# Down projection of the last 1024 tokens: 12 of 28 K tiles by Strassen's scheme for three of four token pairs

## The chip, the cores and the metric

The kernel runs on one core of one Trainium2 chip. The metric is the device time of one execution in microseconds. A core has TensorE (PE in the profile; matmuls, and PEld for the loads of their stationary operand), VectorE (DVE), ScalarE (ACT), GpSimd (POOL) and SyncE (SP, which here issues nearly all DMA transfers). Each engine works off its own queue in order. SBUF is the working memory, PSUM the memory that matmuls write, eight banks of 512 float32 columns.

## The reference

One transformer block on 2048 tokens of width 1024: a conditioned layer norm, linear attention, and a gated FFN of width 3584, both with residuals. What the change touches is the last product.

```python
def _B_ref(x, w_gate, w_up, w_down):
    return _gelu(x @ w_gate) * (x @ w_up) @ w_down

x = x + ga * _A_ref(h, A_wqkv, A_wo)
h = _layernorm(x, axis=-1) * (1 + cb) + sb
x = x + gb * _B_ref(h, B_w_gate, B_w_up, B_w_down)      # w_down: 3584 x 1024, bfloat16
```

## The kernel before

**Tiling.** The 2048 tokens are 16 chunks of 128 (`c_`). The FFN works in two passes `p` of eight chunks each (1024 tokens). A pass has 14 units `u`; a unit makes two of the 28 tiles `fc` (128 wide) of the hidden width, for 1024 tokens, and leaves them in `YT` (bf16). A unit already uses Strassen's scheme in Winograd's form: seven products `P1` to `P7`, each in two halves `t` (gate, up) of four matmuls. P1 and P2 are bf16; P5, P6, P7, P3 and P4 work on sums of operands in float32 that TensorE reads as `f32r`. VectorE makes the sums of the tokens (`s_sum`, line 1371, once a pass) and of the weights (`t_sum`, line 1391, for the next unit); ScalarE converts one more (`A22R`, line 1357, and line 1380). In PSUM, P1 opens a bank, ScalarE copies it to a second bank (`pcp`, line 1421), P6 and P7 add to the copy, and VectorE adds the copy and P5 (`padd`, line 1427, with P5 in `ES`). Then Gelu (line 1432, ScalarE, into `GE`) and the product with the other half (line 1436, VectorE, into `YT`).

**Down projection.** After the units of a pass, `down` (line 1501) multiplies `YT` with `w_down`, which comes in seven groups `WDT[q]` of four K tiles (1 MB each; `wd_dma`, line 1325). Group 2 is loaded in unit 12, groups 5, 3, 6, 4 at the end of a pass, each as soon as the tile it overwrites has been read; groups 0 and 1 stay from the first pass. A chunk takes two banks (`2 * (c_ % 4)`, 512 columns each) and 28 matmuls for each. `evac` (lines 1493, 1494, 1496) multiplies by `GBB`, adds the residual in `XALL` and writes the result to memory.

In the second pass the first four chunks go together, group by group; the next three go one after the other, all 28 K tiles each; the last chunk goes in column pieces of 512, 320, 128 and 64:

```python
                for c_ in gb_[:-1]:
                    down_q(c_, range(7), first=True, last=True)
                c_ = NCH - 1
                for k, (b, k0, k1) in enumerate(((6, 0, 512), (7, 512, 832), (0, 832, 960), (1, 960, 1024))):
                    down(c_, k, b, k0, k1, list(range(NFC)), True, True)
                    evac(c_, k, b, k0, k1)
```

**What sets the order.** Every instruction is recorded by `sch.op` with the bytes that it reads and writes; from these the waits between engines are made. The order on each engine's queue is the order in which the program records, except in one early segment that a planner (`reorder`) sorts, and which ends in the second unit of the first pass. SBUF is one arena with offsets by hand, and tiles overlay each other: `SS` (sums of tokens), `TP` (sums of weights), `WT`, `H2`, `GE`, `ES` belong to the FFN, `XALL` holds the tokens' residuals and results.

Of the kernel before, what the change touches and what calls it, by code (L numbers as in the profile page):

```python
# [6 lines left out]
dt = mybir.dt  # L7
# [3 lines left out]
P = 128  # L11
# [50 lines left out]
OFF_XL = [OFF_GUH + i * 2048 for i in range(4)]  # L62
NXR = 7
OFF_KVT = OFF_GUH + 2048


class Op:
# [246 lines left out]
def bass_adaLN_cond__linear_attn_block__geglu_ffn__prompt_kernel(  # L314
# [16 lines left out]
    with ExitStack() as es:  # L331
# [6 lines left out]
        def at(name, shape, dty, off):  # L338
            return nc.alloc_sbuf_tensor_at(name, shape, dty, offset=ABASE + off, align_bytes=4)
# [22 lines left out]
        W2 = at("w2", [P, NG, D], bf16, OFF_WK)  # L362
        WDQ = [HBO[1], HBO[2], OFF_WS, OFF_WS + 8192, HBO[0], OFF_TP[0], OFF_TP[2]]
        WDT = [at(f"wd{q}", [P, 4, D], bf16, WDQ[q]) for q in range(7)]
        PK = [at(f"pk{i}", [P, D], bf16, OFF_PK[i]) for i in range(NCH)]
        MB = [at(f"mb{i}", [P, D], bf16, OFF_MB[i]) for i in range(NG)]
        MTB = [at(f"mtb{i}", [P, NDC, P], bf16, OFF_MTB[i]) for i in range(2)]
# [136 lines left out]
        def yrow(fc):  # L504
            return fc + 16 if fc < 12 else fc - 12
# [723 lines left out]
        def pq_scale(sg, h, gs):  # L1229
            i, t0 = sg % 2, h * HW  # L1230
            for g0, g1 in gs:
                ap = PQ[sg][:, g0:g1, t0:t0 + HW]
                rng = r_pq(sg, g0, g1, t0, t0 + HW)
                sch.op(V, lambda e, ap=ap, i=i, h=h, g0=g0, g1=g1: e.tensor_tensor(ap, ap, RB[i][:, h, g0:g1, :], ALU.mult),  # L1234
                       rd=rng + r_rb(i, h, g0, g1), wr=rng, deps=rb_ops[sg, h], note=f"pqs{sg}.{h}.{g0}")
# [100 lines left out]
        def ln2_stats(c_, on_act):  # L1336
            i = c_ % 4
            if on_act:
                ln_stats_act(c_, XL[i], r_2k(OFF_XL[i], f"xl{i}"), 1)
            else:  # L1340
                ln_stats(c_, "B")
                ln_nm(c_)

        def ln2_rows(c_):
            i = c_ % 4
            b_, rng = XL[i], r_2k(OFF_XL[i], f"xl{i}")
            xhat_act(c_, b_, rng)
            h, ci = divmod(c_ % (2 * CPG), CPG)
            tdma(Q, H2[h][:, :, ci * P:(ci + 1) * P], b_[:, :], rng, r_h2(h, 0, NDC, ci * P, (ci + 1) * P), f"T2 {c_}")
# [10 lines left out]
        def s_sum(p, i, j):  # L1360
            a, b = H2
            k0, k1, s0, s1 = (2 * j, 2 * j + 2, 0, SGW) if i == 3 else (0, ND2, j * 2 * P, (j + 1) * 2 * P)
            lo = lambda t_: (t_[:, k0:k1, s0:s1])
            hi = lambda t_: (t_[:, ND2 + k0:ND2 + k1, s0:s1])
            rl = lambda h: r_h2(h, k0, k1, s0, s1)
            rh = lambda h: r_h2(h, ND2 + k0, ND2 + k1, s0, s1)
            in0, in1, op, rd = ((lo(b), hi(b), ALU.add, rl(1) + rh(1)),
                                (lo(S32[0]), lo(a), ALU.subtract, r_ss(0, k0, k1, s0, s1) + rl(0)),
                                (lo(a), lo(b), ALU.subtract, rl(0) + rl(1)),
                                (hi(a), lo(S32[1]), ALU.subtract, rh(0) + r_ss(1, k0, k1, s0, s1)))[i]  # L1370
            sch.op(V, lambda e: e.tensor_tensor(SS[i][:, k0:k1, s0:s1], in0, in1, op), rd=rd, wr=r_ss(i, k0, k1, s0, s1), note=f"ssum{i} {p}.{j}")  # L1371
# [63 lines left out]
        def y_out(i, b, fc, h):  # L1435
            sch.op(V, lambda e: e.tensor_tensor(YT[:, yrow(fc), h * SGW:(h + 1) * SGW], GE[i][:, :], PS(b + 1), ALU.mult),  # L1436
                   rd=r_2k(OFF_GE[i], f"ge{i}"), prd=pr(b + 1), wr=r_yt(fc, h * SGW, (h + 1) * SGW), note="yT")
# [3 lines left out]
        def unit(p, u, order=(1, 5, 6, 2, 7, 3, 4)):  # L1441
            more = u + 1 < NFP
            f1, f2 = 2 * u, 2 * u + 1
            done = set()
            for k in order:
                if isinstance(k, tuple):
                    wo_chunk(*k)
                    continue
                if callable(k):
                    k()  # L1450
                    continue
                late = p == u == 0 and k == 2
                gb_, gk, yf, yh = (None, 1, 0, 0) if late else {2: (BA, 0, f1, 0), 7: (BE, 1, f2, 1), 3: (BC, 0, f2, 0), 4: (BB, 0, f1, 1)}.get(k, (None, 1, 0, 0))
                for t in range(2):
                    prod(u, t, k)
                    if k == 1:
                        if held[0]:
                            held[0]()
                            held[0] = None
                        pcp(t)  # L1460
                    elif k == 5:
                        escp(t)
                    elif k == 6:
                        padd(t, BC)
                    elif k == 7:
                        padd(t, BE)
                    if gb_ is not None and t == gk:
                        gelu(gb_)
                        ig = (gi[0] - 1) % 2
                done.add(k)  # L1470
                if k == 2 and u + 2 < NFP:
                    wt_dma(u + 2)
                if k == 4:
                    held[0] = lambda: y_out(ig, BB, f1, 1)
                elif gb_ is not None:
                    y_out(ig, gb_, yf, yh)
                if k == 1:
                    if p == u == 0:
                        ar_copy(0)
                    elif u > 0:  # L1480
                        t_sum(u, 4)
                if more:
                    if k == (3 if p == u == 0 else 5):
                        t_sum(u + 1, 0)
                    if k == (3 if p == u == 0 else 2):
                        t_sum(u + 1, 1)
                    if k == 3:
                        t_sum(u + 1, 3)
                        t_sum(u + 1, 2)
# [24 lines left out]
                    evac(c_, k, b + k, k * 512, (k + 1) * 512)  # L1514

        pq_scale(2, 0, GH[0] + GH[1])
        mark.append(sch.n)
        def cb1():
            sch.op(V, lambda e: e.tensor_scalar(CB1T[:, :], CBT[:, :], 1.0, None, op0=ALU.add), rd=r_sm("cbT"), wr=r_sm("cb1T"))
# [15 lines left out]
        for c_ in range(2, 14):  # L1535
# [4 lines left out]
            if c_ < 10:  # L1540
                ln2_rows(c_ - 2)
            SLOT[c_]()
        ORD0 = (1, 2, 5, 6, lambda: (s_sum(0, 2, 1), gelu(BA)), (14, BE),
                lambda: (y_out(0, BA, 0, 0), s_sum(0, 3, 0), s_sum(0, 3, 1)), 7, (15, BA), 3, 4)
        for p in range(2):
            c0 = p * 2 * CPG
            for u in range(NFP):
                unit(p, u, *([ORD0] if p == u == 0 else []))
                if p == 0 and u == 1:
                    mark.append(sch.n)  # L1550
                if p == 0 and u in (2, 4):
                    wd_dma(u // 2 - 1)
                if u == NFP - 2:
                    wd_dma(2)
            held[0]()
            held[0] = None
            for q in (5, 3, 6, 4):
                wd_dma(q)
            ga_, gb_ = range(c0, c0 + CPG), range(c0 + CPG, c0 + 2 * CPG)
            for c_ in (c0, c0 + 3, c0 + 1, c0 + 2):  # L1560
                down_q(c_, (0,), first=True)
            for q in (1, 2, 3, 5):
                for c_ in ga_:
                    down_q(c_, (q,))
            if p == 0:
                for c_ in range(2 * CPG, NCH):
                    ln2_stats(c_, False)
                    ln2_rows(c_)
                    if c_ == 3 * CPG - 1:
                        mod2_act(0)  # L1570
                    if c_ == NCH - 3:
                        mod2(1, 0, 2)
            for c_ in ga_:
                down_q(c_, (6, 4), last=True)
            if p == 0:
                mod2(1, 2, 2)
                for i, j in ((0, 0), (0, 1), (1, 0), (1, 1), (2, 0), (2, 1), (3, 0), (3, 1)):
                    s_sum(1, i, j)
                for c_ in gb_:
                    down_q(c_, (2, 3), first=True)  # L1580
                wt_dma(0)
                wt_dma(1)
                for q in (4, 5, 6):
                    for c_ in gb_:
                        down_q(c_, (q,))
                    if q == 4:
                        ar_copy(1)
                for k in range(5):
                    t_sum(0, k)
                for c_ in gb_:  # L1590
                    down_q(c_, (0, 1), last=True)
            else:
                for c_ in gb_[:-1]:
                    down_q(c_, range(7), first=True, last=True)
                c_ = NCH - 1
                for k, (b, k0, k1) in enumerate(((6, 0, 512), (7, 512, 832), (0, 832, 960), (1, 960, 1024))):
                    down(c_, k, b, k0, k1, list(range(NFC)), True, True)
                    evac(c_, k, b, k0, k1)


        sch.reorder(mark[0], mark[1], (DVE_, ACT_, POOL_), {id(x4_op): 8.0})
# [73 lines left out]
```

## Time and profile before

| | us |
|---|---|
| median of 3 runs (lowest, highest) | 801.89 (801.64, 802.12) |
| the profiled execution, its own time | 801.02 |
| its span, first to last instruction | 798.9 |
| granted TensorE clock, mean over the span | 1.00 of full speed |
| VectorE busy from 700 to 799 us, by tens | 0, 0, 0, 3.9, 7.3, 1.8, 2.4, 2.8, 1.6, 3.3 |
| TensorE busy from 700 to 799 us, by tens | 10 in each, 6.0 in the last 9 us |
| ScalarE busy from 700 to 799 us | 0 |

A group's duration is that of one instruction from its start to its end. Matmuls overlap, so their spacing is shorter than their duration; it is read from a stretch of the chain of waits, divided by the count. The chain of waits follows the run back from its last instruction, at each step to what released it.

### The profile page before, as it was taken

Reading aid. Unit: us, or ns where it says so; the run is one execution under the profiler, and the core shown is the slowest. Engines: PE = TensorE matmul, PEld = TensorE weight load, DVE = VectorE, ACT = ScalarE, POOL = GpSimd, SP = SyncE. Lnnn points to the kernel's source line nnn. Section 1 sums busy time; section 2 is a strip of 40 time slices with the busy share of each in tenths; the row PEclk is TensorE's granted clock in tenths of the full one; section 3 lists DMA queues with packets and bytes.
Section 4 is the critical chain, followed back from the end, with each engine's and each line's share of the span. In section 5 each row is a group of like instructions: output and inputs, shape, how many; then the busy total and the mean of one; then the engine's idle time right before and its main releaser. Section 6 shows DMA issues by size and latency. Waiting matters only on the chain.

```text
span 798.9 us, 10878 instructions
## 1 busy us (share of the span) xinstructions
PE 792.2 (99%) x4029; PEld 466.0 (58%) x4029; DVE 568.5 (71%) x1008; ACT 302.9 (38%) x511; POOL 40.3 (5%) x102
## 2 busy tenths in 40 slices
PE   8999999999999999999999999999999999999998
PEld 4444445665445776777765444467677777744445
DVE  6799898884989987878876373578887878601422
ACT  2597743232573444435443401034444435300000
POOL 2131200000410000000001000000000000000000
PEclk9999999999999999999999999999999999999999
DMA  9789849849996153323319234023132332430100
GB/s 285 242 179 231 176 110 237 201 95 200 225 268 166 54 158 105 106 71 89 102 56 250 39 80 106 27 80 105 54 105 58 102 90 68 144 120 7 53 21 27
DMA packets 161340, 97.73 MB, mean 122 GB/s; under 512 B 68476, under 2 KB 148612, under 8 KB 160264
## 3 DMA queue, kind: packets, MB, share of 16 engines
q1 hardware_dynamic: 161272, 97.04, 47.4%
q8 instruction: 32, 0.52, 0.3%
q14 instruction: 20, 0.16, 0.1%
q10 hardware_dynamic: 16, 0.00, 0.0%
HBM read 78.92 MB, written 4.47 MB: 104 GB/s over the span
## 4 chain that ended last, share of the span: by engine, by line
PE 92%; DVE 3%; DMA 2%; SPq 1%; issue 1%; ACT 0%; POOL 0%; POOLq 0%; DVEq 0%
PE ps_all L1416 44%; PE ps_all L1501 24%; PE ps_all L873 7%; PE ps_all L909 7%; PE ps_all L858 7%; PE ps_all L1242 2%; DMA wmq<-in_w_mod_dram 1%; DVE xall L1256 1%; DMA wt<-in_B_w_up_dram 1%; SPq L680 1%; DVE tp L1391 0%; PE ps_all L891 0%; PE ps_all L1174 0%; PE ps_all L744 0%; DVE pq L1234 0%
## 5 line engine op out<-in xcount | busy, mean ns | idle before, releaser
L1416 PE MATMUL ps_all<-ss,tp 128*128 128x512 f32 x896 | 224.3, 402 | 0.2 <-DVE ss L1371 0.2
L1501 PE MATMUL ps_all<-wd,yT 128*128 128x512 bf16 (+3 forms) x952 | 193.9, 366 | 0.0
L1416 PEld LDWEIGHTS ps_all<-ss,tp 128*128 128x128 f32 x896 | 168.3, 188 | 40.8 <-DVE ss L1371 0.9
L1501 PEld LDWEIGHTS ps_all<-wd,yT 128*128 128x128 bf16 x952 | 90.0, 98 | 103.8 <-ACT ge L1432 0.5
L1432 ACT ACTIVATE ge<-ps_all 128x512 f32<-128x512 f32 x112 | 64.2, 598 | 143.7 <-DVE ps_all L1427 80.2
L1416 PE MATMUL ps_all<-h2a,wt 128*128 128x512 bf16 x448 | 106.2, 380 | 0.0
L1391 DVE TENSOR_TENSOR tp<-wt 128x512 fp32r<-128x512 bf16 x112 | 74.5, 689 | 41.9 <-PE ps_all L1416 20.6
L1436 DVE TENSOR_TENSOR yT<-ge,ps_all 128x512 bf16<-128x512 f32 x112 | 74.6, 685 | 34.3 <-PE ps_all L1416 30.9
L1427 DVE TENSOR_TENSOR ps_all<-ps_all,es 128x512 f32<-128x512 f32 x112 | 75.3, 696 | 16.0 <-PE ps_all L1416 16.0
L1493 DVE TENSOR_TENSOR ps_all<-ps_all,gbb 128x512 f32<-128x512 f32 (+3 forms) x34 | 22.7, 668 | 79.0 <-PE ps_all L1501 79.0
L1391 DVE TENSOR_TENSOR tp<-wt,tp 128x512 fp32r<-128x512 bf16 x112 | 72.1, 685 | 0.0
L1416 PEld LDWEIGHTS ps_all<-h2a,wt 128*128 128x128 bf16 x448 | 39.4, 98 | 54.3 <-issue 13.9
L858 PE MATMUL ps_all<-wk,h1T 128*128 128x512 bf16 x248 | 56.7, 379 | 0.4 <-DVE h1T L701 0.4
L909 PE MATMUL ps_all<-h1T,wq 128*128 128x512 bf16 x256 | 56.7, 379 | 0.0
L1242 PE MATMUL ps_all<-w,pq 128*128 128x512 bf16 x256 | 56.3, 379 | 0.0
L1416 PE MATMUL ps_all<-ar,tp 128*128 128x512 f32 x224 | 55.3, 389 | 0.0
L1421 ACT ACTIVATE ps_all<-ps_all 128x512 f32<-128x512 f32 x56 | 32.6, 582 | 55.3 <-PE ps_all L1416 53.2
L847 ACT ACTIVATE eb<-ps_all 128x512 f32<-128x512 f32 x64 | 36.4, 593 | 36.8 <-PE ps_all L858 13.8
L1416 PEld LDWEIGHTS ps_all<-ar,tp 128*128 128x128 f32 x224 | 42.0, 188 | 8.7
L909 PEld LDWEIGHTS ps_all<-h1T,wq 128*128 128x128 bf16 x256 | 25.0, 98 | 30.0
L1242 PEld LDWEIGHTS ps_all<-w,pq 128*128 128x128 bf16 x256 | 24.7, 98 | 29.9 <-ACT w L1176 0.3
L858 PEld LDWEIGHTS ps_all<-wk,h1T 128*128 128x128 bf16 x248 | 23.7, 98 | 28.8 <-DVE h1T L701 2.2
(118 smaller groups left out, 650.3 us busy)
## 6 DMA issues: line engine op xcount, KB each, us to landing
wt<-in_B_w_gate_dram SPq DMA_DIRECT2D x28, 512.0 KB, 4.1
wt<-in_B_w_up_dram SPq DMA_DIRECT2D x28, 512.0 KB, 4.9
wd<-in_B_w_down_dram SPq DMA_DIRECT2D x12, 1024.0 KB, 7.2
rb<-scr_rd SPq DMA_DIRECT2D x32, 256.0 KB, 6.2
wmst<-in_w_mod_dram SPq DMA_DIRECT2D x6, 1024.0 KB, 5.7
wmq<-in_w_mod_dram SPq DMA_DIRECT2D x8, 512.0 KB, 6.4
out_dram<-xall SPq DMA_DIRECT2D x31, 128.0 KB, 1.7
xall<-in_A_x_dram SPq DMA_DIRECT2D x5, 512.0 KB, 5.4
```

Source lines behind the costliest of these rows:

```text
L847: sch.op(A, lambda e: e.activation(EB[i][:, :], PS(bank), ACTF.Exp), prd=pr(bank), wr=rng, note=f"{note}.exp")
L858: o = sch.op(T, lambda e, dc=dc: e.matmul(PS(bank), H1[sg][:, ci, dc, :], W_[:, dc, jg * 512:(jg + 1) * 512], start=(dc == 0), stop=(dc == ...
L873: o = sch.op(T, lambda e, c_=c_: e.matmul(PS(bank, 0, n), PK[c_][:, g * P:(g + 1) * P], xrow(c_, o_, o_ + n), start=(c_ == 0), stop=(c_ == ...
L909: o = sch.op(T, lambda e, dc=dc: e.matmul(PS(b), WQ[:, dc, qc * P:(qc + 1) * P], H1[sg][:, :, dc, :], start=(dc == 0), stop=(dc == NDC - 1 ...
L1242: last[half] = sch.op(T, lambda e, g=g, half=half: e.matmul(PS(b0 + half), PQ[sg][:, g, ci * P:(ci + 1) * P], W2[:, g, half * 512:(half + ...
L1391: sch.op(V, lambda e, t=t: e.tensor_tensor(TP[k][:, t, :, :], in0[:, t, :, :], in1[:, t, :, :], ALU.subtract), rd=r0[t:t + 1] + (r1[t:t + ...
L1416: o = sch.op(T, lambda e, l_=l_, r_=r_, dc=dc: e.matmul(PS(b), l_, r_, start=fresh and dc == 0, stop=dc == ND2 - 1, skip_group_check=True) ...
L1421: sch.op(A, lambda e: e.activation(PS(BB + t), PS(BA + t), ACTF.Copy), prd=pr(BA + t), pwr=pr(BB + t), note="pcp")
L1427: sch.op(V, lambda e: e.tensor_tensor(PS(dst + t), PS(BB + t), ES[t][:, :], ALU.add), prd=pr(BB + t), rd=r_2k(OFF_ES[t], f"es{t}"), pwr=pr ...
L1432: sch.op(A, lambda e: e.activation(GE[i][:, :], PS(b), ACTF.Gelu_apprx_tanh), prd=pr(b), wr=r_2k(OFF_GE[i], f"ge{i}"), note="gelu")
L1436: sch.op(V, lambda e: e.tensor_tensor(YT[:, yrow(fc), h * SGW:(h + 1) * SGW], GE[i][:, :], PS(b + 1), ALU.mult), rd=r_2k(OFF_GE[i], f"ge{i ...
L1501: o = sch.op(T, lambda e, fc=fc: e.matmul(PS(b, 0, n), YT[:, yrow(fc), ci * P:(ci + 1) * P], WDT[fc // 4][:, fc % 4, c0:c1], start=first a ...
```

## The change

For the second pass, the first two chunks (8 and 9) run the plain down projection alone, in four banks. For the pairs (10, 11), (12, 13) and (14, 15) the first 12 K tiles are done by the scheme that the FFN uses, on blocks of [two token chunks] x [two K tiles of 128] x [two halves of 512 columns], six such blocks of K (`NDJ = 6`). A block's eight plain matmuls become seven. The other 16 K tiles are added as before. New are:

- `d_t(q, i)`: sums of the weights of group `q` (0 to 2), four on VectorE and one conversion on ScalarE, 128 x 1024 in f32r each. Those of group 0 are put between the products of the last unit of the second pass (`ORD1`), the others after it. They lie where the FFN's sums, its tokens, `GE`, `ES` and the finished results of the first tokens lay (`OFF_DT`).
- `d_s(ca, cb, i)`: sums of `YT` for a pair, four on VectorE and one conversion on ScalarE, 128 x 768; three of them lie in the halves of the weight groups 0 to 2 that the scheme does not read any more (`DH`).
- `d_prod`, `d_add`, `d_pair`: the seven products in four banks, with ScalarE's copies of P1 and P5 and VectorE's adds; then the next pair's sums, then the rest of the K tiles and `evac`.

The last pair keeps the pieces of 512, 320, 128 and 64 columns for its second chunk, now for the last 16 K tiles; `TAIL` puts the sums of the products into three banks.

```diff
+NDJ = 6
+OFF_DT = [[OFF_XALL, OFF_XALL + 4096, OFF_R3, OFF_R3 + 4096, OFF_R3 + 8192],
+          [OFF_R3 + 12288, OFF_HT + 24576, OFF_HT + 28672, OFF_R3 + 16384, OFF_R3 + 20480],
+          [OFF_GUH, OFF_GUH + 4096, OFF_R3 + 24576, OFF_ROW, OFF_GAB]]
+OFF_DS = [OFF_XALL + 8192, OFF_XALL + 8192 + NDJ * 512]
+OFF_DE = OFF_XALL + 8192 + NDJ * 1024
...
+        DH = [at("dha", [P, 4, 2, 512], f32r, HBO[1]), at("dhb", [P, 2, 2, 512], f32r, OFF_WS)]
...
+        def d_t(q, i):
+            w = WDT[q].ap().rearrange("p (j r) d -> p j r d", r=2)
+            b = lambda r, cc: w[:, :, r, cc * 512:(cc + 1) * 512]
...
+            if i == 3:
+                sch.op(A, lambda e: e.activation(DT[q][3][:], b(1, 1), ACTF.Copy), rd=rb_(1, 1), wr=r_dt(q, 3), note=f"dtcp {q}")
+                return
+            in0, in1, rd = ((b(0, 1), b(0, 0), rb_(0, 1) + rb_(0, 0)), (b(1, 1), t32(0), rb_(1, 1) + r_dt(q, 0)),
+                            (b(1, 1), b(0, 1), rb_(1, 1) + rb_(0, 1)), None, (b(1, 0), t32(1), rb_(1, 0) + r_dt(q, 1)))[i]
+            sch.op(V, lambda e: e.tensor_tensor(DT[q][i][:], in0, in1, ALU.subtract), rd=rd, wr=r_dt(q, i), note=f"dtsum {q}.{i}")
...
+        def d_s(ca, cb, i):
+            for j0, j1 in (((0, NDJ),) if i < 2 else ((0, 4), (4, NDJ))):
+                dst, wr = ds_ap(i, j0, j1)
+                if i == 4:
+                    src, rd = y_ap(cb, 1, j0, j1)
+                    sch.op(A, lambda e, dst=dst, src=src: e.activation(dst, src, ACTF.Copy), rd=rd, wr=wr, note=f"dscp {cb}")
+                    continue
...
+                sch.op(V, lambda e, dst=dst, in0=in0, in1=in1, op=op: e.tensor_tensor(dst, in0, in1, op), rd=r0 + r1, wr=wr, note=f"dssum{i} {cb}")
+
+        def d_prod(ca, b0, k):
+            b = b0 + {1: 0, 2: 0, 5: 3, 6: 2, 7: 2, 4: 2, 3: 1}[k]
+            o = None
+            for j in range(NDJ):
+                if k in (1, 2):
+                    l_, rl = y_ap(ca, k - 1, j, j + 1)
+                    fc = 2 * j + k - 1
+                    r_, rr = WDT[fc // 4][:, fc % 4, 0:512], [(WDQ[fc // 4] + fc % 4 * 2048, WDQ[fc // 4] + fc % 4 * 2048 + 1024, f"wd{fc // 4}")]
+                else:
...
+                o = sch.op(T, lambda e, l_=l_, r_=r_, j=j: e.matmul(PS(b), l_[:, 0, :], r_, start=k in (1, 5) and j == 0, stop=j == NDJ - 1, skip_group_check=True),
+                           rd=rl + rr, pwr=(pr(b) if j == 0 else ()), note=f"down P{k} c{ca} j{j}", overwrite_ok=True)
+            pset_writer(b, o)
...
+        def d_add(b0, parts):
+            for b, c0, c1 in parts:
+                sch.op(V, lambda e, b=b, c0=c0, c1=c1: e.tensor_tensor(PS(b, 0, c1 - c0), PS(b0 + 2, c0, c1), DE[:, c0:c1], ALU.add),
+                       prd=pr(b0 + 2), rd=R_DE, pwr=pr(b), note="dpadd")
+
+        TAIL = ((7, 0, 320), (0, 320, 448), (1, 448, 512))
+
+        def d_pair(ca, nxt):
+            b0 = 2 * (ca % CPG)
+            for k in (1, 5, 6, 2, 7, 3, 4):
+                d_prod(ca, b0, k)
+                if k == 1:
+                    sch.op(A, lambda e: e.activation(PS(b0 + 2), PS(b0), ACTF.Copy), prd=pr(b0), pwr=pr(b0 + 2), note="dpcp")
+                elif k == 5:
+                    sch.op(A, lambda e: e.activation(DE[:, :], PS(b0 + 3), ACTF.Copy), prd=pr(b0 + 3), wr=R_DE, note="descp")
+                elif k == 6:
+                    d_add(b0, ((b0 + 1, 0, 512),))
+                elif k == 7:
+                    d_add(b0, ((b0 + 3, 0, 512),) if nxt else TAIL)
+            if nxt:
+                for i in range(5):
+                    d_s(ca + 2, ca + 3, i)
+                for q in (3, 5, 6, 4):
+                    for c_ in (ca, ca + 1):
+                        down_q(c_, (q,), last=q == 4)
+                return
+            fcs = list(range(2 * NDJ, NFC))
+            for k in range(2):
+                down(ca, k, b0 + k, k * 512, (k + 1) * 512, fcs, False, True)
+                evac(ca, k, b0 + k, k * 512, (k + 1) * 512)
+            for k, (b, k0, k1) in enumerate(((b0 + 2, 0, 512),) + tuple((b, c0 + 512, c1 + 512) for b, c0, c1 in TAIL)):
+                down(ca + 1, k, b, k0, k1, fcs, False, True)
+                evac(ca + 1, k, b, k0, k1)
...
+        ORD1 = (1, lambda: d_t(0, 0), 5, lambda: d_t(0, 1), 6, 2, lambda: d_t(0, 2), 7, 3, lambda: (d_t(0, 3), d_t(0, 4)), 4)
...
-                unit(p, u, *([ORD0] if p == u == 0 else []))
+                unit(p, u, *([ORD0] if p == u == 0 else [ORD1] if p and u == NFP - 1 else []))
...
+            if p:
+                for q, i in [(1, i) for i in range(5)] + [(2, i) for i in range(5)]:
+                    d_t(q, i)
+                for q in (0, 1, 2):
+                    for c_ in (c0, c0 + 1):
+                        down_q(c_, (q,), first=q == 0)
+                for i in range(5):
+                    d_s(c0 + 2, c0 + 3, i)
+                for q in (5, 3, 6, 4):
+                    for c_ in (c0, c0 + 1):
+                        down_q(c_, (q,), last=q == 4)
+                for c_ in (c0 + 2, c0 + 4, c0 + 6):
+                    d_pair(c_, c_ + 2 < NCH)
+                break
...
-            else:
-                for c_ in gb_[:-1]:
-                    down_q(c_, range(7), first=True, last=True)
-                c_ = NCH - 1
-                for k, (b, k0, k1) in enumerate(((6, 0, 512), (7, 512, 832), (0, 832, 960), (1, 960, 1024))):
-                    down(c_, k, b, k0, k1, list(range(NFC)), True, True)
-                    evac(c_, k, b, k0, k1)
```

More of the change, by code (lines that the diff above doesn't have):

```diff
@@ L364, in bass_adaLN_cond__linear_attn_block__geglu_ffn__prompt_kernel @@
         WDT = [at(f"wd{q}", [P, 4, D], bf16, WDQ[q]) for q in range(7)]
+        DT = [[at(f"dt{q}{i}", [P, 2, 512], f32r, OFF_DT[q][i]) for i in range(5)] for q in range(3)]
+        DS = [at(f"ds{i}", [P, NDJ, P], f32r, OFF_DS[i]) for i in range(2)]
+        DE = at("de", [P, 512], f32, OFF_DE)
+        DH = [at("dha", [P, 4, 2, 512], f32r, HBO[1]), at("dhb", [P, 2, 2, 512], f32r, OFF_WS)]
         PK = [at(f"pk{i}", [P, D], bf16, OFF_PK[i]) for i in range(NCH)]
@@ L1516, in bass_adaLN_cond__linear_attn_block__geglu_ffn__prompt_kernel, with r_dt @@
         pq_scale(2, 0, GH[0] + GH[1])
+        def r_dt(q, i):
+            return [(OFF_DT[q][i], OFF_DT[q][i] + 4096, f"dt{q}{i}")]
+        def d_t(q, i):
+            w = WDT[q].ap().rearrange("p (j r) d -> p j r d", r=2)
+            b = lambda r, cc: w[:, :, r, cc * 512:(cc + 1) * 512]
+            rb_ = lambda r, cc: [(WDQ[q] + (2 * j + r) * 2048 + cc * 1024, WDQ[q] + (2 * j + r) * 2048 + (cc + 1) * 1024, f"wd{q}") for j in range(2)]
+            t32 = lambda k: DT[q][k].ap().bitcast(f32)
+            if i == 3:
[4 more added lines that the diff above has]
+            sch.op(V, lambda e: e.tensor_tensor(DT[q][i][:], in0, in1, ALU.subtract), rd=rd, wr=r_dt(q, i), note=f"dtsum {q}.{i}")
@@ new lines, in bass_adaLN_cond__linear_attn_block__geglu_ffn__prompt_kernel, with ds_ap @@
+        DHS = {2: (0, 0), 3: (0, 1), 4: (1, 0)}
+        def ds_ap(i, j0, j1):
+            if i < 2:
+                return DS[i][:, j0:j1, :], [(OFF_DS[i] + j0 * 512, OFF_DS[i] + j1 * 512, f"ds{i}")]
+            r, sl = DHS[i]
+            h, o_, base = (0, 0, HBO[1]) if j1 <= 4 else (1, 4, OFF_WS)
+            return (DH[h][:, j0 - o_:j1 - o_, r, 256 + sl * P:256 + (sl + 1) * P],
+                    [(base + (2 * (j - o_) + r) * 2048 + 1024 + sl * 512, base + (2 * (j - o_) + r) * 2048 + 1536 + sl * 512, f"dh{i}") for j in range(j0, j1)])
@@ new lines, in y_ap @@
+        def y_ap(c_, r, j0, j1):
+            ci = c_ % (2 * CPG)
+            r0 = yrow(2 * j0 + r)
+            return (YT[:, r0:r0 + 2 * (j1 - j0) - 1:2, ci * P:(ci + 1) * P], [t_ for j in range(j0, j1) for t_ in r_yt(2 * j + r, ci * P, (ci + 1) * P)])
+        def d_s(ca, cb, i):
[5 more added lines that the diff above has]
+                    continue
+                s_ = lambda k: (ds_ap(k, j0, j1)[0].bitcast(f32), ds_ap(k, j0, j1)[1])
+                (in0, r0), (in1, r1), op = ((y_ap(cb, 0, j0, j1), y_ap(cb, 1, j0, j1), ALU.add), (s_(0), y_ap(ca, 0, j0, j1), ALU.subtract),
+                                            (y_ap(ca, 0, j0, j1), y_ap(cb, 0, j0, j1), ALU.subtract), (y_ap(ca, 1, j0, j1), s_(1), ALU.subtract))[i]
+                sch.op(V, lambda e, dst=dst, in0=in0, in1=in1, op=op: e.tensor_tensor(dst, in0, in1, op), rd=r0 + r1, wr=wr, note=f"dssum{i} {cb}")
@@ new lines, in d_prod @@
+        def d_prod(ca, b0, k):
[7 more added lines that the diff above has]
+                else:
+                    l_, rl = ds_ap({5: 0, 6: 1, 7: 2, 3: 3, 4: 4}[k], j, j + 1)
+                    ti = {5: 0, 6: 1, 7: 2, 3: 3, 4: 4}[k]
+                    r_, rr = DT[j // 2][ti][:, j % 2, :], [(OFF_DT[j // 2][ti] + j % 2 * 2048, OFF_DT[j // 2][ti] + j % 2 * 2048 + 2048, f"dt{j // 2}{ti}")]
+                o = sch.op(T, lambda e, l_=l_, r_=r_, j=j: e.matmul(PS(b), l_[:, 0, :], r_, start=k in (1, 5) and j == 0, stop=j == NDJ - 1, skip_group_check=True),
+                           rd=rl + rr, pwr=(pr(b) if j == 0 else ()), note=f"down P{k} c{ca} j{j}", overwrite_ok=True)
+            pset_writer(b, o)
@@ new lines, in bass_adaLN_cond__linear_attn_block__geglu_ffn__prompt_kernel @@
+        R_DE = [(OFF_DE, OFF_DE + 2048, "de")]
+        def d_add(b0, parts):
[29 more added lines that the diff above has]
+                evac(ca + 1, k, b, k0, k1)
@@ L1564, in bass_adaLN_cond__linear_attn_block__geglu_ffn__prompt_kernel @@
                     down_q(c_, (q,))
[L1565 to L1572, printed above, removed]
+            for c_ in range(2 * CPG, NCH):
+                ln2_stats(c_, False)
+                ln2_rows(c_)
+                if c_ == 3 * CPG - 1:
+                    mod2_act(0)
+                if c_ == NCH - 3:
+                    mod2(1, 0, 2)
             for c_ in ga_:
                 down_q(c_, (6, 4), last=True)
[L1575 to L1578, printed above, removed]
-                for c_ in gb_:
[L1580 to L1591, printed above, removed]
-            else:
-                for c_ in gb_[:-1]:
-                    down_q(c_, range(7), first=True, last=True)
-                c_ = NCH - 1
-                for k, (b, k0, k1) in enumerate(((6, 0, 512), (7, 512, 832), (0, 832, 960), (1, 960, 1024))):
-                    down(c_, k, b, k0, k1, list(range(NFC)), True, True)
-                    evac(c_, k, b, k0, k1)
+            mod2(1, 2, 2)
+            for i, j in ((0, 0), (0, 1), (1, 0), (1, 1), (2, 0), (2, 1), (3, 0), (3, 1)):
+                s_sum(1, i, j)
+            for c_ in gb_:
+                down_q(c_, (2, 3), first=True)
+            wt_dma(0)
+            wt_dma(1)
+            for q in (4, 5, 6):
+                for c_ in gb_:
+                    down_q(c_, (q,))
+                if q == 4:
+                    ar_copy(1)
+            for k in range(5):
+                t_sum(0, k)
+            for c_ in gb_:
+                down_q(c_, (0, 1), last=True)
         sch.reorder(mark[0], mark[1], (DVE_, ACT_, POOL_), {id(x4_op): 8.0})
```

## The prediction

> **What bounds the kernel now.** I first read the busy times, then the chain of waits over the second half of the run.
>
> ```profile
> PE 792.2 (99%) x4029; PEld 466.0 (58%) x4029; DVE 568.5 (71%) x1008; ACT 302.9 (38%) x511; POOL 40.3 (5%) x102
> ```
>
> ```profile
> 426.03 96.71 PE ps_all L1501 x448
> 522.74 176.38 PE ps_all L1416 x784
> 699.12 96.86 PE ps_all L1501 x504
> 795.99 0.02 issue
> 796.01 0.24 DVE ps_all L1493
> ```
>
> Columns of the second view: start, length, what. TensorE works from 426 us to 796 us without a wait: a down projection, the FFN of the last 1024 tokens, their down projection. So any matmul taken out of the last stage is worth its spacing, and a wait put before one costs its length. The spacings follow from the counts. Down, bf16: 96.71 / 448 = 0.2159 us. FFN: 224 of the 784 are bf16 (two of seven products), 48.4 us; the rest leaves 128.0 / 560 = **0.2286 us for an f32r matmul**, 6% more.
>
> The timeline of TensorE in the last FFN unit shows that this is no wait, but the pace of f32r:
>
> ```profile
> 686.36 1.90 PE L1416 MATMUL ps_all<-h2a,wt 128*128 128x512 bf16 x8
> 687.91 4.00 PE L1416 MATMUL ps_all<-ss,tp 128*128 128x512 f32 x16
> 691.76 1.90 PE L1416 MATMUL ps_all<-h2a,wt 128*128 128x512 bf16 x8
> 693.31 4.00 PE L1416 MATMUL ps_all<-ss,tp 128*128 128x512 f32 x16
> ```
>
> Columns: start, length, instructions. The unit's period is the same as in all the others, 176.38 / 14 = 12.60 us. VectorE in the same unit is the engine with least room:
>
> ```profile
> 687.37 1.29 DVE L1391 TENSOR_TENSOR tp<-wt,tp 128x512 fp32r<-128x512 bf16 x2
> 691.12 0.70 DVE L1427 TENSOR_TENSOR ps_all<-ps_all,es 128x512 f32<-128x512 f32 x1 [2.45 <-PE ps_all L1416]
> 692.01 0.70 DVE L1427 TENSOR_TENSOR ps_all<-ps_all,es 128x512 f32<-128x512 f32 x1 [0.19 <-PE ps_all L1416]
> 693.76 0.69 DVE L1436 TENSOR_TENSOR yT<-ge,ps_all 128x512 bf16<-128x512 f32 x1 [1.06 <-PE ps_all L1416]
> 694.61 0.70 DVE L1427 TENSOR_TENSOR ps_all<-ps_all,es 128x512 f32<-128x512 f32 x1 [0.16 <-PE ps_all L1416]
> ```
>
> The brackets are idle time before the instruction. The last unit prepares no weights for a next one, so it has a gap of 2.45 us where the new sums go. After 700 us VectorE is nearly free: 23.7 us busy of the last 99.
>
> **Term 1: the matmuls.** In each of three token pairs 12 K tiles x 2 tokens x 2 halves = 48 bf16 matmuls, 48 x 0.2159 = 10.36 us, become seven products of six: P1 and P2 in bf16, 12 x 0.2159 = 2.59, and five in f32r, 30 x 0.2286 = 6.86. That is 9.45 us, **0.91 us less for a pair, 2.74 us for three**. The f32r spacing contains the entry into a block of f32r, two for 40 in the FFN, two for 30 here: an inner block of eight runs at 1.81 / 8 = 0.2263 (684.55 to 686.36 us), so an entry is 40 x 0.0023 / 2 = 0.05 us and the denser entries add 0.03 a pair, 0.09 in all. Bounds: if f32r ran here at the bf16 spacing, 1.14 us more gain; at 3.85 / 16 = 0.2406, the start to start of one block above, 1.08 us less. I take the FFN's mean, since stationary and moving tiles have the same shape there.
>
> The Trainium skill ("TensorE: Matmul & The Clock Gate", Back-to-back issue gap) gives N/2.4 + 2.5 ns, 216 ns at 512 columns, with no word on the operand's type. By that rule the change would be worth, as an estimate, 18 x 0.216 = 3.9 us; the bf16 rows agree with it, the f32r rows (0.2286) do not, and I go by the rows.
>
> **Term 2: the last token chunk.** It runs in pieces of 512, 320, 128 and 64 columns: 96.86 - 392 x 0.2159 = 12.24 us against 12.09 for 56 plain ones. For 12 of 28 tiles that overhead goes: -0.06.
>
> **Term 3: the end.** The last writes on VectorE:
>
> ```profile
> 793.63 0.50 DVE L1493 TENSOR_TENSOR ps_all<-ps_all,gbb 128x320 f32<-128x320 f32 x1 [2.38 <-PE ps_all L1501]
> 794.16 0.49 DVE L1494 TENSOR_TENSOR xall<-ps_all,xall 128x320 bf16<-128x320 f32 x1
> 795.19 0.30 DVE L1493 TENSOR_TENSOR ps_all<-ps_all,gbb 128x128 f32<-128x128 f32 x1 [0.54 <-PE ps_all L1501]
> 795.53 0.29 DVE L1494 TENSOR_TENSOR xall<-ps_all,xall 128x128 bf16<-128x128 f32 x1
> 796.01 0.23 DVE L1493 TENSOR_TENSOR ps_all<-ps_all,gbb 128x64 f32<-128x64 f32 x1 [0.19 <-PE ps_all L1501]
> ```
>
> VectorE waits 0.54 and 0.19 us for the two short pieces. They now have 16 tiles, not 28: 12 x 0.056 = 0.67 us and 12 x 0.029 = 0.35 us less. So TensorE's end comes 1.02 us nearer, VectorE's only by its 0.73 us of waiting: +0.29. The three output transfers come closer together too (the 80 KB one lands 3.3 us after issue); from 0 to 0.5 more, I take 0.
>
> **Term 4: the hand-overs inside a pair.** These are new: TensorE must wait for ScalarE's copy of P1 before P6, for VectorE's first add before P7 and P3, for its second before P4. A matmul ends 0.16 us after the next starts (0.38 long). ScalarE begins 0.04 us after the block of 686.36 ends (688.26 to 688.30), VectorE 0.10 us after that of 687.91 (691.91 to 692.01); the way back is 0.04 (a sum of SS ends at 245.73, TensorE starts at 245.77). Copy: 0.16 + 0.04 + 0.58 + 0.04 = 0.82 us under P5's 1.37. Add: 0.16 + 0.10 + 0.70 + 0.04 = 1.00 under P2's 1.30, then under P3's 1.37. In the last pair the second add is cut in three, 0.50 + 0.30 + 0.23 and two gaps: 1.39 under 1.37. VectorE must be free by then: the eight writes of the preceding pair (four banks of 1.39 us) begin 2.4 us before the pair and end 3.2 us into it; the first add is due at 4.3. So +0.05; bounds 0 and, with 0.1 lost at each of twelve, 1.2. No gain is possible here.
>
> **Costed at nothing, and what hides it.** *Weight sums.* 12 VectorE sums of 1024 columns at 1.22 us (the FFN's sums of the tokens) and 3 ScalarE copies at 1.05. Two of them come before the add due at 691.12: VectorE is free at 688.66, + 2.44 = 691.10. It just fits. The third holds back the two adds after P7 by about 1.1 us, to 695.7 and 696.4; P4 needs the banks at 697.15 and 698.05. The Gelu behind those adds and its product slip by about 1 us, which nobody awaits: the down projection opens with banks 0 to 3, the last of which is free near 697.7 and needed at 700.7. The fourth ends near 699.6 and delays the last product of the FFN by 0.4 us, read by the sixth group of K tiles at 716 us. Eight sums remain after the FFN: about 700.3 to 710.1. *Operand sums of tokens* for the first pair: 768 columns, 0.95 us between the rows of 512 (0.69) and 1024 (1.22), twice, and twice 0.69 + 0.43: 4.1 us, to 714.3. TensorE reaches that pair after 112 matmuls, at 699.0 + 24.2 = 723.1, so 9 us are to spare. Later pairs make them under 64 matmuls, 13.8 us. If this cover went, it would be 14 us on the path. *Weights of the down projection.* Two tokens instead of four pass each group, so groups 5, 3, 6, 4 are needed at 709.3, 712.8, 716.2 and 719.7. Their transfers go out at 692.00, 693.73, 697.34 and 699.15, take 8.7 us at most, and the DMA's busy share is 0.01 from 710 us on. *SP's queue:* the same writes of the output, the first ones 14 us earlier, with nothing behind them. The order on POOL is unchanged.
>
> **The sum.** -2.74 + 0.09 - 0.06 + 0.29 + 0.05 = **-2.4 us**. The profiled execution took 801.02 us, its span 798.9 with 2.1 around it; it would become 798.6. The median of the runs is 801.89, so the forecast is **799.5 us**. What this kernel's measurement can tell from no change is about 0.2%, 1.6 us; the line is at 800.3.
>
> **Rivals.** *A: VectorE in the last FFN unit is late.* The weight sums read with a stride of 4 KB between tiles; if they took twice 1.22 us, the first two would end at 693.5 and the adds at 694.2, 0.7 us after P7 wants the bank, and some of it again after the third. Against it: the FFN's own weight sums read strided too, at 0.69. Price 0.8 to 1.5 us, so about 800.6: no change that can be told. *B: the hand-overs decide, slower.* Within a pair one block of six covers each, where the FFN has three half products of four, some 2.6 us. At twice the time of the rows the copy takes 1.64 (0.3 over its cover), the adds 2.0 (0.7 and 0.6 over): 1.6 us a pair, 4.8 us in all, 799.5 + 4.8 = **804.3**. It eats the gain from 0.8 us a pair on and is slower by over 0.2% from 1.3. For it: VectorE has 5.6 us of output writes around each pair's start, only 1 us clear of the first add. Against: every row used is of the same instruction on the same banks. *C: f32r at the bf16 spacing here*, 798.4; nothing in the FFN's rows speaks for it. That the products are not what they seem, more than 42 a pair, would show in the count alone; the loops give 42.
>
> **How the numbers follow.** Forecast 0.70, A with other small stalls 0.17, B 0.08, C 0.05. Faster by over 0.2%: forecast and C, 0.75; the same: A, 0.17; slower: B, 0.08. The forecast's own range is 798.8 to 800.3. The whole range reaches down to C's value and up through A, 798.4 to 801.2, leaving out B and a little more.
>
> **What would show it.** The chain should still be TensorE alone from 523 us to the end, its last stage near 94.2 us with 462 matmuls instead of 504 (18 by the scheme, 24 by 12 tiles that are no longer cut in four pieces), 90 of them f32r at 0.227 to 0.23. The last FFN unit should keep its 12.6 us. ScalarE's copies and VectorE's adds within pairs should have no TensorE idle time behind them. Wrong would be: idle TensorE before P6, P7 or P4 (B), a longer last unit (A), or an f32r spacing other than 0.2286 (term 1).

## The result and the profile after

| | before | after |
|---|---|---|
| median, us (lowest to highest of 6 runs each) | 801.95 (801.64 to 802.12) | 798.57 (797.85 to 799.10) |
| profiled execution, its own time / its span | 801.02 / 798.9 | 798.54 / 796.3 |

The ratio of the runs is 0.9958, with a 95% interval of 0.9946 to 0.9971: faster by 2.3 to 4.3 us. Forecast were 799.5 us for the median and 798.6 for the profiled execution.

The busy times of the changed kernel:

```profile
PE 789.3 (99%) x3987; PEld 470.2 (59%) x3987; DVE 595.8 (75%) x1046; ACT 312.2 (39%) x526; POOL 40.4 (5%) x102
```

TensorE has 42 matmuls less, VectorE 38 instructions more, and the share of TensorE is the same. The chain of waits (start, length, what) from the second FFN on:

```profile
523.00 176.38 PE ps_all L1426 x784
699.38 24.19 PE ps_all L1511 x112
723.57 9.50 PE ps_all L1581 x42
733.07 13.83 PE ps_all L1511 x64
746.90 9.50 PE ps_all L1581 x42
756.41 13.83 PE ps_all L1511 x64
770.24 9.50 PE ps_all L1581 x42
779.74 12.56 PE ps_all L1511 x64
```

The FFN takes 176.38 us as before, so the sums put into its last unit cost nothing (rival A). The plain pair takes 112 x 0.216 us. Each pair's seven products (line 1581) take 9.50 us where 48 plain matmuls took 10.36. No piece of another engine stands between them until the last evacuations. VectorE in the last FFN unit (start, length, instruction, idle time before it):

```profile
688.83 1.22 DVE L1540 TENSOR_TENSOR dt<-wd 128x1024 fp32r<-128x1024 bf16 x1
690.08 1.23 DVE L1540 TENSOR_TENSOR dt<-wd,dt 128x1024 fp32r<-128x1024 bf16 x1
691.37 0.70 DVE L1437 TENSOR_TENSOR ps_all<-ps_all,es 128x512 f32<-128x512 f32 x1
692.28 0.70 DVE L1437 TENSOR_TENSOR ps_all<-ps_all,es 128x512 f32<-128x512 f32 x1 [0.21 <-PE ps_all L1426]
694.02 0.69 DVE L1446 TENSOR_TENSOR yT<-ge,ps_all 128x512 bf16<-128x512 f32 x1 [1.04 <-PE ps_all L1426]
694.63 1.22 DVE L1540 TENSOR_TENSOR dt<-wd 128x1024 fp32r<-128x1024 bf16 x1
695.76 1.29 DVE L1437 TENSOR_TENSOR ps_all<-ps_all,es 128x512 f32<-128x512 f32 x2
```

The two sums fill the gap of 2.45 us that stood before the add at 691.12; this execution runs 0.26 us later, and the add comes at 691.37, so on time. The third sum holds the two adds after P7 back, to 695.76, and nobody misses them. The end on VectorE:

```profile
792.33 0.50 DVE L1503 TENSOR_TENSOR ps_all<-ps_all,gbb 128x320 f32<-128x320 f32 x1 [0.75 <-PE ps_all L1511]
792.86 0.49 DVE L1504 TENSOR_TENSOR xall<-ps_all,xall 128x320 bf16<-128x320 f32 x1
793.27 0.29 DVE L1503 TENSOR_TENSOR ps_all<-ps_all,gbb 128x128 f32<-128x128 f32 x1
793.59 0.29 DVE L1504 TENSOR_TENSOR xall<-ps_all,xall 128x128 bf16<-128x128 f32 x1
793.80 0.22 DVE L1503 TENSOR_TENSOR ps_all<-ps_all,gbb 128x64 f32<-128x64 f32 x1
794.05 0.22 DVE L1504 TENSOR_TENSOR xall<-ps_all,xall 128x64 bf16<-128x64 f32 x1
```

The waits of 0.54 and 0.19 us are gone, as forecast: VectorE works through the last pieces without a pause. A write that had to wait for TensorE started 0.04 us after it (TensorE's last matmul before ends at 795.97, the write starts at 796.01). A short piece that is ready starts 0.08 us before the preceding write ends (793.27 against 792.86 + 0.49, 793.80 against 793.59 + 0.29), so the end lost little.

### The profile page after: what moved, and what is told of

Its sections match the earlier page's. It is cut to its first block, busy times and chain, and to the rows that moved or that the text cites. A ratio compares the mean times of both kernels' runs of the same rounds, so it can differ in the third digit from the quotient of the medians.

```text
span 796.3 us, 10865 instructions
## 1 busy us (share of the span) xinstructions
PE 789.3 (99%) x3987; PEld 470.2 (59%) x3987; DVE 595.8 (75%) x1046; ACT 312.2 (39%) x526; POOL 40.4 (5%) x102
## 4 chain that ended last, share of the span: by engine, by line
PE 94%; DVE 2%; SPq 2%; DMA 1%; issue 0%; DVEq 0%
PE ps_all L1426 44%; PE ps_all L1511 20%; PE ps_all L883 7%; PE ps_all L919 7%; PE ps_all L868 6%; PE ps_all L1252 5%; PE ps_all L1581 4%; SPq L585 1%; DMA wmq<-in_w_mod_dram 1%; DVE xall L1266 1%; SPq L590 1%; DVE tp L1401 0%; PE ps_all L901 0%; PE ps_all L1184 0%; DVE ss L1381 0%
## 5 line engine op out<-in xcount | busy, mean ns | idle before, releaser
L1511 PE MATMUL ps_all<-wd,yT 128*128 128x512 bf16 (+3 forms) x784 | 163.3, 370 | 0.0
L1511 PEld LDWEIGHTS ps_all<-wd,yT 128*128 128x128 bf16 x784 | 74.7, 98 | 87.8 <-issue 0.8
L857 ACT ACTIVATE eb<-ps_all 128x512 f32<-128x512 f32 x64 | 36.3, 593 | 36.9 <-PE ps_all L868 14.2
L1434 ACT ACTIVATE es<-ps_all 128x512 f32<-128x512 f32 x56 | 33.5, 601 | 18.3 <-PE ps_all L1426 17.3
```

What stands on the lines that cost most here:

```text
L857: sch.op(A, lambda e: e.activation(EB[i][:, :], PS(bank), ACTF.Exp), prd=pr(bank), wr=rng, note=f"{note}.exp")
L1434: sch.op(A, lambda e: e.activation(ES[t][:, :], PS(BE + t), ACTF.Copy), prd=pr(BE + t), wr=r_2k(OFF_ES[t], f"es{t}"), note="escp")
L1511: o = sch.op(T, lambda e, fc=fc: e.matmul(PS(b, 0, n), YT[:, yrow(fc), ci * P:(ci + 1) * P], WDT[fc // 4][:, fc % 4, c0:c1], start=first a ...
```

## The experiments

A yardstick first. The times of single executions scatter by more than the terms in question, but one stretch does not: from the start of the second FFN to the end of the last write on VectorE, both read from the chain of waits. The last write of the kernel before is this piece of its chain:

```profile
796.28 0.22 DVE xall L1494
```

So the stretch is 796.50 - 522.74 = 273.76 us before and 794.27 - 523.00 = **271.27** after: the change is worth 2.49 us there. The table has this stretch for every kernel.

| kernel | stretch, us | start of the second FFN | median, us | ratio (95%) |
|---|---|---|---|---|
| before | 273.76 | 522.74 | 801.95 | |
| after | 271.27 | 523.00 | 798.57 | 0.9958 (0.9946 to 0.9971) |
| e1, before again | 273.77 | 523.48 | 801.24 | 0.9999 (0.9990 to 1.0008) |
| e2, after again | 271.28 | 523.13 | 798.72 | 0.9964 (0.9951 to 0.9976) |
| e3, order alone | 273.76 | 523.30 | 801.53 | 1.0000 (0.9991 to 1.0009) |
| e4, bf16 sums | 269.91 | 522.59 | 796.79 | 0.9943 (0.9929 to 0.9956) |
| e5, adds twice | 274.36 | 523.63 | 802.05 | 1.0003 (0.9994 to 1.0012) |
| e6, sums late | 271.28 | 522.86 | 798.82 | 0.9962 (0.9950 to 0.9975) |
| e7, FFN in bf16 too | 262.73 | 515.15 | 782.11 | 0.9755 (0.9741 to 0.9768) |
| e8, short extra add | 271.52 | 523.29 | 798.57 | 0.9962 (0.9950 to 0.9975) |

The kernel before ran beside e1 to e4 with a median of 801.40 (21 runs), beside e5 to e7 with 801.56 (15), beside e8 with 801.65 (9).

**e1 and e2: both kernels once more, unchanged.** The medians had moved by 3.4 us, the profiled executions by 2.5.

> The kernel before, unchanged, against itself. Open is why the medians moved by 3.4 us (801.95 to 798.57) where the two traces account for 2.5 (profiled executions 801.02 and 798.54). Theory 1 (scatter of the early part, before 246 us, from one execution to the next; the profiled execution of before was an early one): ratio 1.000, the six or more times spread over about 1 us, and in a new profile the FFN of the second pass starts some tenths later than 522.74 us, up to 523.7, with everything after it as before: 176.38 us and 96.86 us. Theory 2 (the change also shortens something ahead of the last stage): start near 522.7 again, and the missing 0.9 us is found elsewhere.

> The changed kernel, unchanged, once more. Theory 1: ratio between 0.9955 and 0.9972 (2.3 to 3.6 us), start of the second FFN anywhere from 522.5 to 523.7 us, last stage from the end of the FFN to the last write on VectorE 94.9 us as before (97.4 in the kernel before). Theory 2: the start of the second FFN lies earlier in every execution of this kernel than in those of the kernel before.

The chain of e1, its first FFN piece of the second pass and its last write:

```profile
523.48 5.38 PE ps_all L1416 x24
...
797.02 0.23 DVE xall L1494
```

Measured: 801.24 and 798.72 us; the stretches repeat to 0.01 us. The second FFN starts anywhere from 522.59 to 523.63 us over nine profiles (all but e7's), with no order by kernel. Theory 1 holds for the start. A second part was in neither theory: from the last write to the end of the span the kernel before and its likes take 2.4, 2.0 and 2.5 us (before, e1, e3), the changed one and its likes 2.0 or 2.1 each time (after, e2, e6, e8). The 80 KB transfer near the end lands 3.3, 2.8 and 3.4 us after its issue in before, e1 and e3, and 1.6 in the others. So behind the stretch the change gains up to half a us more, and against e1 nothing; e2's median is 2.7 us under the 801.40 beside it.

The traces point at a cause. In before, e1 and e3 one packet of 0.02 MB of the DMA queue that the profile lists as "q8 instruction" runs while this transfer is under way; within one microsecond it takes 8.7, 6.0 and 9.7% of 16 engines' time, that is 1.39, 0.96 and 1.55 us on one engine, in the same order as the landing times. In the changed kernel and its likes the last such packet runs about 20 us earlier. No run moves this packet alone, so the cause is argued, not shown.

**e3: the order alone.** Pairs of tokens, but no scheme; all 28 K tiles plain.

```diff
+            if nxt:
+                for q in (0, 1, 2, 3, 5, 6, 4):
+                    for c_ in (ca, ca + 1):
+                        down_q(c_, (q,), first=q == 0, last=q == 4)
+                return
+            fcs = list(range(NFC))
...
+            return
             for k in (1, 5, 6, 2, 7, 3, 4):
                 d_prod(ca, b0, k)
...
-                unit(p, u, *([ORD0] if p == u == 0 else [ORD1] if p and u == NFP - 1 else []))
+                unit(p, u, *([ORD0] if p == u == 0 else []))
...
-                for q, i in [(1, i) for i in range(5)] + [(2, i) for i in range(5)]:
-                    d_t(q, i)
...
-                for i in range(5):
-                    d_s(c0 + 2, c0 + 3, i)
```

> The order of the change alone: token pairs, group by group, but all 28 K tiles as plain bf16 matmuls, no operand sums, no copies and adds. My sum gives the order nothing: last stage 504 matmuls in 96.9 us, the end as in the kernel before (28 tiles in the short pieces, VectorE waits for them again), ratio 0.999 to 1.001. Rival (part of the gain is the order, earlier output writes): 0.3 to 1 us faster than before.

Measured: ratio 1.0000, stretch 273.76. The order is worth nothing; earlier output writes are worth nothing either. All of the 2.49 us belongs to the scheme.

**e4: the price of f32r.** The down projection's sums in bf16.

```diff
-        DT = [[at(f"dt{q}{i}", [P, 2, 512], f32r, OFF_DT[q][i]) for i in range(5)] for q in range(3)]
-        DS = [at(f"ds{i}", [P, NDJ, P], f32r, OFF_DS[i]) for i in range(2)]
+        DT = [[at(f"dt{q}{i}", [P, 2, 512], bf16, OFF_DT[q][i]) for i in range(5)] for q in range(3)]
+        DS = [at(f"ds{i}", [P, NDJ, P], bf16, OFF_DS[i]) for i in range(2)]
...
```

> The changed kernel with the sums of weights and tokens, and so the five products on sums, in bf16 instead of float32 read as f32r (the products of the first 12 K tiles become less exact; nothing is left out). Term 1 says that 90 matmuls go from 0.2286 to 0.2159 us: 42 products in 9.07 us a pair instead of 9.50, 1.3 us less in all, about 797.3, ratio to before 0.9942. Rival (the f32r spacing is set by the block changes or by what ScalarE and VectorE write meanwhile, not by the type): the block stays at 9.4 to 9.5 us and the time at 798.6.

The chain of e4 over the first pair:

```profile
723.16 1.29 PE ps_all L1581 x6
724.46 0.05 issue
724.51 7.72 PE ps_all L1581 x35
732.23 3.02 PE ps_all L1511 x14
```

From 723.16 to 732.23 the 42 products (one record is missing) take 9.07 us, to the hundredth what the bf16 spacing gives, against 9.50. The stretch is 1.36 us shorter for 1.3 expected. The median fell by 1.9 against e2; in the two profiled executions most of the rest is an earlier start of the FFN (522.59 against 523.13). The sums written meanwhile are not behind the spacing either: from the first matmul of P1 to that of P2 VectorE makes no sum in either kernel, and this part shrank from 4.07 us (723.41 to 727.48 in the changed kernel) to 3.88 (723.00 to 726.88). The f32r spacing is the type's.

The Trainium skill ("TensorE: Matmul & The Clock Gate", Back-to-back issue gap) has 216 ns for 512 columns, as the gap of an isolated matmul. The products of e4, 9.07 / 42 = 0.216 us, agree with this figure, and f32r lies 6% above it. The same section gives about 131 ns for a sustained stream of loads and matmuls; no run here comes near that, and the measurement decides.

**e5: how much cover the hand-overs have.** Each add of VectorE twice.

```diff
                 elif k == 6:
                     d_add(b0, ((b0 + 1, 0, 512),))
+                    d_add(b0, ((b0 + 1, 0, 512),))
                 elif k == 7:
                     d_add(b0, ((b0 + 3, 0, 512),) if nxt else TAIL)
+                    d_add(b0, ((b0 + 3, 0, 512),) if nxt else TAIL)
```

> The changed kernel with each of VectorE's two adds of a pair made twice (the second writes the same values). It tests term 4: how much cover the hand-overs have. In the trace of the changed kernel the first add ends 0.34 us before P7 starts, the second 0.48 before P4, the three pieces of the last pair 0.35; a second add adds 0.61 us. Cover theory: waits of about 0.3 a pair at P7, 0.17 at P4 in two pairs and 0.35 in the last, 1.6 us in all, about 800.3. Rival B (the adds are on the path already): in full, 6 x 0.61 = 3.7 us, about 802.4. Third theory (much more cover than that): no change, 798.7.

The chain of e5 in the first pair, with VectorE on it:

```profile
728.38 0.71 DVE ps_all L1589
729.09 0.02 issue
729.11 0.71 DVE ps_all L1589
729.82 0.04 issue
729.87 1.67 PE ps_all L1581 x6
```

Measured: the stretch grew by 3.09 us, twice what I expected and near the rival that had the adds on the path already. They were not (e2 has no such wait); two sizes were wrong. A second add to the same bank costs 729.11 - 728.38 = 0.73 us, not 0.61: it starts 0.02 us after the first has ended, where adds into different banks overlap. And the cover is shorter than I took it: pairs come every 24.32 us (724.21 to 748.53) instead of 23.33, so of 2 x 0.73 us only 0.47 was covered, where the prediction has 0.30 + 0.37.

**e8: where the cover ends.** Run after e5, to see why.

```diff
                 elif k == 6:
+                    d_add(b0, ((b0 + 1, 0, 64),))
                     d_add(b0, ((b0 + 1, 0, 512),))
```

> The changed kernel with a short extra add (64 columns, about 0.25 us) before the first add of each pair. It tells two readings of the cover apart that e5 left. Mine in the prediction: P7 needs its bank when its first matmul starts, after six matmuls of P2, 1.30 us, 0.30 to spare: no change, 271.27 us from the start of the second FFN to the last write on VectorE. The new one: the wait stands before the load of the first stationary tile, which goes out with P2's sixth matmul, so the cover is five matmuls, 1.08 us, 0.08 to spare: about 0.17 us lost in each pair, 0.5 us in all, 271.8 us; the load of P7's first tile starts 0.05 us after the add's end.

The timeline of the changed kernel and then of e8 at the first add, with the loads of stationary tiles (PEld):

```profile
727.74 0.70 DVE L1589 TENSOR_TENSOR ps_all<-ps_all,de 128x512 f32<-128x512 f32 x1 [1.30 <-PE ps_all L1581]
...
728.57 0.19 PEld L1581 LDWEIGHTS ps_all<-dt,dha 128*128 128x128 f32 x1
728.59 0.58 PE L1581 MATMUL ps_all<-dt,dha 128*128 128x512 f32 x1
```

```profile
728.04 0.97 DVE L1589 TENSOR_TENSOR ps_all<-ps_all,de 128x64 f32<-128x64 f32 x2 [1.30 <-PE ps_all L1581]
729.06 0.30 PEld L1581 LDWEIGHTS ps_all<-dt,dha 128*128 128x128 f32 x2 [0.31 <-DVE ps_all L1589]
```

In the changed kernel the load of P7's first tile goes out at 728.57 with P2's sixth matmul, 0.13 us after the add's end at 728.44. In e8 the adds end at 729.01 and the load follows at 729.06: it stands behind the wait, as the new reading says. Counted from the first load of P2 (727.47 in the changed kernel, 727.77 in e8) it goes out 1.29 instead of 1.10 us later, so it is 0.19 us late; the extra add took 0.27 us, and 0.08 were to spare up to the load, as that reading has it. But the price was half of what it gave: 0.25 us in the stretch, 0.08 a pair. So 0.11 of the 0.19 us stayed hidden, under P2's last matmul as far as the timeline tells. In terms of time lost, 0.19 us were to spare: less than the 0.30 of the prediction, more than the 0.08 of my second reading. Neither had the price right.

**e6: the sums' place.** Group 0 after the FFN as well.

```diff
-                unit(p, u, *([ORD0] if p == u == 0 else [ORD1] if p and u == NFP - 1 else []))
+                unit(p, u, *([ORD0] if p == u == 0 else []))
...
-                for q, i in [(1, i) for i in range(5)] + [(2, i) for i in range(5)]:
+                for q, i in [(q, i) for q in range(3) for i in range(5)]:
```

> The changed kernel with the weight sums of group 0 after the FFN like those of groups 1 and 2, none inside the last FFN unit. My sum gives their place nothing: VectorE would make 12 sums and the first pair's operand sums until about 717.3 us, TensorE reaches that pair at 723.6. From the start of the second FFN to the last write on VectorE 271.27 us as in the changed kernel (before: 273.76), ratio as e2. Rival A (the last FFN unit is slowed by them): 0.3 to 1 us less, in the last FFN unit.

Measured: 271.28, no change. Rival A is out: the last unit loses nothing to the sums, and the time after the FFN could hold them as well.

**e7: the FFN's sums in bf16 too.** e4 pointed past the change: the same 6% stand on 1120 matmuls of the FFN.

```diff
-        A22R = at("ar", [P, NDC // 2, SGW], f32r, HBO[0])
-        SS = [at(f"ss{i}", [P, NDC // 2, SGW], f32r, OFF_SS[i]) for i in range(4)]
-        TP = [at(f"tp{i}", [P, 2, NDC // 2, P], f32r, OFF_TP[i]) for i in range(5)]
+        A22R = at("ar", [P, NDC // 2, 2 * SGW], bf16, HBO[0])
+        SS = [at(f"ss{i}", [P, NDC // 2, 2 * SGW], bf16, OFF_SS[i]) for i in range(4)]
+        TP = [at(f"tp{i}", [P, 2, NDC // 2, 2 * P], bf16, OFF_TP[i]) for i in range(5)]
...
```

> The kernel of e4 with the FFN's sums of tokens and weights, and so its five products on sums, in bf16 too (those products become less exact; nothing is left out). If the f32r spacing is the type's, 1120 matmuls go from 0.2286 to 0.2159 us: units of 12.09 us instead of 12.60, 14.2 us less than e4, about 782.6. Rival (in the FFN the f32r spacing is also set by what VectorE and ScalarE do meanwhile, or the hand-overs come on the path in shorter units): units between 12.2 and 12.6 us, 783 to 796.

Groups of the page of e7 (instruction, count, busy time, mean ns of one, idle time before):

```profile
L1426 PE MATMUL ps_all<-ss,tp 128*128 128x512 bf16 x879 | 201.8, 379 | 0.9
L1426 PEld LDWEIGHTS ps_all<-ss,tp 128*128 128x128 bf16 x896 | 87.7, 98 | 105.7
...
L1401 DVE TENSOR_TENSOR tp<-wt 128x512 bf16<-128x512 bf16 x112 | 44.7, 421 | 67.2 <-PE ps_all L1426 40.5
```

Measured: 782.11 us, 14.7 below e4 for 14.2 expected; the stretch, which holds one of the two passes, is 7.18 us shorter, 560 x 0.0128. This version beats both kernels, at the price of sums rounded to bf16. VectorE's sums fell too, from 689 to 421 ns, which the path does not see: the 14 units take 169.22 us (515.15 to 684.37), 12.09 each, as the bf16 spacing alone gives.

## Why the prediction was right

**The mechanism** is the one forecast: TensorE alone sets the time, fewer matmuls at its spacing are the gain, every sum is hidden. 2.49 us came in the stretch where the sum had 2.37.

**Term 1** was right to 0.1 us: a pair's products take 9.50 us, the sum had 9.45 + 0.03; three pairs gain 2.59, not 2.65. Going by the f32r rows rather than by one spacing for all types decided the forecast; by the latter it would have been 3.9.

**Term 2**, the pieces of the last chunk, does not show: TensorE's part of the stretch, up to the end of its last matmul (795.97 before, 793.65 after), is 2.58 us shorter, as much as the three pairs give.

**Term 3** was mis-sized. VectorE's end lies 0.62 us behind TensorE's (793.65 to 794.27) instead of 0.53 (795.97 to 796.50): +0.09, not +0.29. I had added up durations; a short piece that is ready overlaps the write before by 0.08 us, twice. And the output transfers, put at 0 with a bound of 0.5 more, went the other way: up to 0.5 less. No step of the sum forecast that; it is luck. The bound was one-sided where the row of 3.3 us for the 80 KB transfer, far longer than the 1.7 of the larger ones, should have raised the question.

**Term 4** had the right value, about nothing, from a cover that was too large: "Add: 0.16 + 0.10 + 0.70 + 0.04 = 1.00 under P2's 1.30". The add itself took that long, but 0.19 us were to spare (e8), not 0.30, for the wait for the bank holds more than the product's first matmul: its weight load waits too, 0.19 us long for float32 (728.57). With e5, 0.47 - 0.19 = 0.28 remain at the second add, where I had 0.37. Rival B was therefore nearer than the prediction says; doubled adds alone take the whole gain back.

The Trainium skill (the same page, "Weight-path perf modes — Fast Weight Load (FWL) and DoubleRow") says that the fast weight load is off for FP32. The loads of 188 ns in f32r (recorded as f32) against 98 in bf16 fit that; that the wait delays the load is shown by e5 and e8.

**The median** moved by 3.4 us, 0.9 more than the profiled executions. No step of the sum stands behind that: the start of the second FFN scatters by 1 us from profile to profile, and the six runs of the kernel before, 801.64 to 802.12, all lay above the median of its 56 later ones (801.47; 800.65 to 803.23). How much of the rest is the earlier end of the transfers, some tenths in the profiles, and how much chance, stays open.

So the number has luck in it. 798.57 lies below the forecast's own range (798.8 to 800.3), within the whole one, and nearer to rival C's 798.4 than to 799.5. C is out all the same: a pair takes 9.50 us, and 9.07 only once the type is bf16 (e4). The profiled execution, 798.54 for 798.6, came out so close because a start 0.26 us later and transfers about 0.4 us earlier almost cancel. The sum is confirmed by the stretch, 2.49 for 2.37, not by either total.

One reading of the prediction was wrong without bearing on the sum: the DMA's busy share is 0.01 or less from 710 us only up to 730; from there the output writes of the kernel before take 0.05 to 0.22 in steps of 10 us. The weights had landed by then.

## What to carry to other kernels

Where TensorE never waits, price an instruction by its spacing in a stretch of the same operand type: here f32r costs 6% over bf16, and a scheme that saves one matmul in eight but turns five of seven into f32r keeps two thirds of its gain. Count the cover of a hand-over up to the start of the next product's weight load. What lies between that and the first matmul covers only in part: here 0.08 us were left to the load, 0.30 by the prediction's count to the matmul, and 0.19 by the price (e8). And measure small changes on a stretch that repeats to 0.01 us rather than on whole executions that scatter by a microsecond.

## What the runs showed that was not expected

- A wait of TensorE on VectorE holds the following weight load back as well: the load comes 0.05 us after the add's end (e5, e8), and of 0.19 us that it came late 0.08 showed in the time (e8).
- Two VectorE adds into the same PSUM bank follow each other every 0.73 us (e5), writes of the same size into different tiles every 0.61 (721.75 to 722.36 in the changed kernel).
- The last output transfers land later in the kernel before: 2.0 to 2.5 us from the last write to the end of the span, 2.0 or 2.1 in the changed one. A packet of the instruction queue beside them fits this; no run isolates it.
- Sums of two bf16 tiles written in bf16 take 0.68 us for 1024 columns on VectorE (e4), written in float32 1.22.
